# Exponentials on VectorE from three shifted bit lines and by single heads, in an attention block on one core

## The chip, the cores and the metric

The kernel runs on one core of one Trainium2 chip. The metric is the device time of one execution in microseconds. A core has five engines that run their own instruction queues in order and meet through semaphores: TensorE (PE in the profile; its weight loads stand apart as PEld), VectorE (DVE), ScalarE (ACT), GpSimd (POOL) and SyncE (SP, which here only issues DMAs). TensorE writes its results to PSUM, eight banks of 128 partitions x 512 f32; VectorE and ScalarE read them there.

## What is computed

A multi-head attention block: 2048 positions, width 448, 16 heads of 28 values.

```python
B, S, D = x.shape          # 1, 2048, 448
H = 16
Dh = D // H                # 28
qkv = (x @ wqkv).reshape(B, S, 3, H, Dh).transpose(2, 0, 3, 1, 4)
q, k, v = qkv[0], qkv[1], qkv[2]
scores = einsum("bhqd,bhkd->bhqk", q, k) * (Dh ** -0.5)
p = softmax(scores, axis=-1)
o = einsum("bhqk,bhkd->bhqd", p, v)
return o.transpose(0, 2, 1, 3).reshape(B, S, D) @ wo
```

Inputs and output are bf16.

## The kernel before

**Tiling.** Four heads form a group g (G = 4); each head has 32 partitions, 28 for its values and four for helper rows. Queries are cut in four chunks c of 512 (QW), keys in 16 tiles j of 128 (NKT). A *set* is one group with one query chunk: 4 heads x 16 key tiles = 64 score tiles of 128 keys x 512 queries. There are 16 sets, worked off in the order of the list ORDER.

**Scores.** `emit_s` (L599) multiplies a key tile with a query chunk. The contraction is 28 values and some helper rows that subtract a bound of the maximum and fold in a constant, so that the result needs no maximum search. TensorE can be addressed as smaller arrays. A score product uses either the 32 rows of its head i, or 64 rows: two heads' rows, where the query tile QP[c][k][z] holds zeros for the other head of the pair. Heads 0 and 1 lie in rows 0 to 63 (half 0), heads 2 and 3 in rows 64 to 127 (half 1). A *step* is a key tile for two heads, hp and hp + 2, one of each half. If a step is emitted alone, its two products take 64 rows each; if ScalarE's and VectorE's steps are emitted together, all four take 32 rows each (the argument `alone`):

```python
r = slice(2 * HP * k, 2 * HP * (k + 1)) if wide(s, t) and alone else slice(HP * i, HP * (i + 1))
```

**Exponentials.** 512 steps are shared out between two engines. ScalarE takes a step from one of two pairs of banks, "a0" and "a1", with its exponential (`do_exp`, L773) and writes the tile pt in bf16. VectorE takes a step from the pair "d" (`do_a`, L785): it adds a constant to the scaled score and stores 16-bit integers I, whose bits read as bf16 are a power of two with a linear mantissa. For two such steps together (2048 columns) `do_add` (L806) makes two terms: m, from the mantissa bits (an and/or, then a product with I itself), and E, the exponent bits alone. Their sum approximates the exponential, so VectorE's steps give two value products for each head, ScalarE's give one. LOGSUM is the constant that puts both on the same scale.

**Value products.** `do_pv` (L866) multiplies the tile VA (32 columns for each head: 28 values and a column of ones that sums the softmax denominator) with a term and adds it up in bank "o". Head i uses columns 32i to 32i + 31 of the array, so the products of the four heads can run side by side; `waves` (L855) pairs a step of heads 0 and 2 with one of heads 1 and 3.

**After a set** (`finish_set`, L904), bank "o" goes to SBUF, the denominators travel through DRAM by DMA to be inverted and spread, and VectorE multiplies. Output projections run through bank "m", as do the projections of K, Q and V of later groups, spread over the sets by gates that count steps.

**Order.** The program's order is decided when it is built, by a planner in the kernel: it keeps a clock for each engine with estimated durations (D_S = 0.325 us for a score step whatever its tile sizes, D_WAVE for four value products, D_EXP for an exponential), and picks for the engine whose clock is lowest. `pick_pe` (L964) prefers a score step as soon as a bank is free, then value products and projections; where TensorE's recent load is low it inserts products on zeros into "o" or "m" (`dense`, L634). `s_choose` (L657) gives VectorE a step beside ScalarE's if `dve_ok` (L649) says that VectorE would be done before ScalarE; it asks that bank "d" has been free for D_LATE = 0.25 us. On the chip the engines keep the order, not the times.

Of the kernel before, what the change touches and what calls it, by code (L numbers as in the profile page):

```python
# [16 lines left out]
LAT = 0.2  # L17
# [6 lines left out]
D_LATE = 0.25  # L24
# [12 lines left out]
def kernel(  # L37
# [29 lines left out]
    NTERM = 2  # L67
    LOGSUM = 0.5864160
# [25 lines left out]
    VA = [[big.tile([P, GH, XB, P], BF16, name=f"VA{h}_{b}") for b in range(NXB)] for h in range(2)]  # L94
    xs = [big.tile([P, XB, D], BF16, name=f"xs{b}") for b in range(NXB)]
# [78 lines left out]
    res = {"a0": 0.0, "a1": 0.0, "d": 0.0, "o": 0.0, "m": 0.0}  # L174
    ops = {"PE": [], "ACT": [], "DVE": [], "SP": []}
    cnt = {"step": 0}
# [9 lines left out]
    def ready(op):  # L186
        if cnt["step"] < op.gate or (op.acq == "m" and op.gives[0][0] == "O" and left() < 6):
            return None
        r = 0.0
        for n in op.need:  # L190
            if n not in evt:
                return None
            t, e = evt[n]
            r = max(r, t + (0.03 if e == op.eng else LATS.get((e, op.eng), LAT)))
        if op.acq is not None:
            if res[op.acq] is None:
                return None
            r = max(r, res[op.acq])
        return r + op.lag
# [42 lines left out]
    def k_job(g, sc, bank, pri, gate=0, split=2, eng="DVE", epri=None):  # L242
# [3 lines left out]
        def mm(part):  # L246
            if part == 0:
                held[key] = bank_tile(bank) if bank in ("o", "m") else pair_tile(bank)
            mm_proj(held[key][:, 0:QW], 1, g, sc, range(part * n, (part + 1) * n))
# [23 lines left out]
    def kn_job(g, bank, pri, gate=0):  # L273
        key = ("KN", g)

        def mm(sc):
            if sc == 0:
                held[key] = bank_tile(bank) if bank in ("o", "m") else pair_tile(bank)
# [22 lines left out]
    def kn_first(sc, bank, pri):  # L301
        key = ("KN0", sc)

        def mm():
            held[key] = pair_tile(bank)[:, 0:QW]
            nc.tensor.matmul(out=held[key], lhsT=blockK[:], rhs=sqt.pop(("K", 0, sc))[:], start=True, stop=True)
# [23 lines left out]
    def q_job(g, c, bank, pri, gate=0, split=2):  # L330
# [4 lines left out]
        def mm(part):  # L335
            if part == 0:
                held[key] = bank_tile(bank) if bank in ("o", "m") else pair_tile(bank)
            mm_proj(held[key][:, 0:QW], 0, g, c, range(part * n, (part + 1) * n))

        def evac():  # L340
            if first:
                t = qtt[0] = wk.tile([P, QW], BF16, name="qt0", bufs=1)
            else:
                t = QAt[(g, c)] = big.tile([P, QW], BF16, name=f"QA{c}", tag=f"QA{c}", bufs=2)
# [27 lines left out]
    def qn_first(bank, pri):  # L372
        g = c = 0

        def mm():
            held["qn0"] = bank_tile(bank) if bank in ("o", "m") else pair_tile(bank)
# [11 lines left out]
        def join():  # L388
            QAt[(0, 0)] = big.tile([P, QW], BF16, name="QA0", tag="QA0", bufs=2)
# [41 lines left out]
    def v_job(h, kt, bank, pri, gate=0, eng="DVE"):  # L431
# [4 lines left out]
        def mm(part):  # L436
            if part == 0:
                held[key] = bank_tile(bank) if bank in ("o", "m") else pair_tile(bank)
# [20 lines left out]

    def oproj_job(c, tq, pri):  # L460
# [9 lines left out]
        def evac():  # L470
            held[key + ("sb",)] = osb = wk.tile([P, D], BF16, name="osb", bufs=3)
# [57 lines left out]
    for b, bank in enumerate(("a0", "a1", "d", "a0")):  # L529
# [4 lines left out]
    for sc in range(NQC):  # L534
        kn_first(sc, "a1" if sc % 2 == 0 else "d", 1.5)
# [9 lines left out]
    for kt in range(0, NKT, 2):  # L545
        v_job(0, kt, "o" if kt in (0, 4) else "m", 7 + kt, eng="ACT" if kt < 6 else "DVE")
    q_job(0, 1, "m", 16.2)
# [5 lines left out]
    for g in range(1, G):  # L553
        a = (g - 1) * NQC * STEPS + (STEPS + 4 if g == 1 else 6)
        z = g * NQC * STEPS - 34 - (STEPS if g == G - 1 else 0)
# [7 lines left out]
    for kt in range(0, NKT, 2):  # L563
        v_job(1, kt, "m", 150 + kt, a + (z - a) * kt // NKT)
    for c in range(CL):
# [4 lines left out]
    remain = {s: [list(range(NKT)), list(range(NKT))] for s in range(NSET)}  # L570
    todo = sum(len(q) for s in remain for q in remain[s])
    started = set()
# [7 lines left out]

    def set_gc(s):
        return ORDER[s]

    def next_step(hp, s_min=0):
        for s in range(s_min, NSET):
            if remain[s][hp]:
                return s
            if s > cur["s"]:
                return None
        return None  # L590
# [5 lines left out]
    def take(s, hp):  # L596
        return (s, hp, remain[s][hp].pop(0))

    def emit_s(ps, off, step, alone, t):  # L599
        s, hp, j = step  # L600
        g, c = set_gc(s)
        q = QP[c][hp][g % 2] if wide(s, t) else QAt[(0, 0)]
        for k in range(2):
            i = hp + 2 * k
            r = slice(2 * HP * k, 2 * HP * (k + 1)) if wide(s, t) and alone else slice(HP * i, HP * (i + 1))
            nc.tensor.matmul(out=ps[:, (off + k) * QW:(off + k + 1) * QW],  # L606
                             lhsT=KAt[(g, j // XB)][r, (j % XB) * P:(j % XB + 1) * P], rhs=q[r, :],
                             start=True, stop=True, tile_position=(r.start, 0))

# [36 lines left out]
    def exp_tail_est():  # L646
        return max(free["ACT"], 0.0) + D_EXP * (len(exps) + left())

    def dve_ok(t):  # L649
        if res["d"] is None or res["d"] > t - D_LATE:  # L650
            return False
        if chain["cur"] is None and chain["used"] >= NCH:
            return False
        fin = max(free["DVE"], t + 0.5) + 1.14 + 3 * 0.34 + 0.3 + (1.8 if adds else 0.0)
        return fin <= free["ACT"] + D_EXP * (len(exps) + max(0, left() - 2)) + 0.2

    def s_choose(t):  # L657
        s = cur["s"]
        while s < NSET and not remain[s][0] and not remain[s][1]:
            s += 1  # L660
        if s >= NSET:
            return None
        cur["s"] = s
        q = qa_ready(s)
        if q is None or q > t:
            return None
        r = remain[s]
        dstep = astep = None
        if dve_ok(t) and left() >= 4:
            ds, want = d_set(s, t)  # L670
            if ds is not None and remain[ds][want] and r[1 - want]:
                dstep, astep = take(ds, want), take(s, 1 - want)
        if astep is None:
            hp = 0 if len(r[0]) > len(r[1]) else 1 if len(r[1]) > len(r[0]) else cur["half"]
            cur["half"] = 1 - hp
            astep = take(s, hp)
        return (None, astep, dstep)

    def d_set(s, t):
        ch = chain["cur"]  # L680
        if ch is not None:
            cs = ch["steps"][0][0]
            if remain[cs][ch["next"]]:
                return cs, ch["next"]
            if remain[cs][1 - ch["next"]]:
                return cs, 1 - ch["next"]
            return None, None
        n = len(remain[s][0]) + len(remain[s][1])
        if n < DRAIN:
            s += 1  # L690
            if s >= NSET:
                return None, None
            q = qa_ready(s)
            if q is None or q > t:
                return None, None
        r = remain[s]
        return s, (0 if len(r[0]) >= len(r[1]) else 1)

    def do_sd(t):
        s = cur["s"]  # L700
        if s >= NSET or not dve_ok(t) or left() < 4:
            return None
        q = qa_ready(s)
        if q is None or q > t:
            return None
        s, want = d_set(s, t)
        if s is None or not remain[s][want]:
            return None
        end = t + D_S
        put_d(take(s, want), end, True, t)  # L710
        note(t, 512 if wide(s, t) else 256)
        cnt["step"] += 1
        return end

    def put_d(dstep, end, alone, t):
        pd = pair_tile("d")
        emit_s(pd, 0, dstep, alone, t)
        outst[dstep[0]] += NTERM
        res["d"] = None
        if chain["cur"] is None:  # L720
            chain["used"] += 1
            chain["cur"] = {"I": wk.tile([P, 4 * QW], I16, name="I4", bufs=NCH), "steps": [], "sh": [], "open": 0,
                            "next": None, "done": 0}
        ch = chain["cur"]
        ch["steps"].append(dstep)
        ch["next"] = 1 - dstep[1]
        a_fifo.append((end + LATS[("PE", "DVE")], pd, ch, len(ch["steps"]) - 1))
        if len(ch["steps"]) == 2:
            chain["cur"] = None
# [4 lines left out]
    def s_ready():  # L734
        if left() == 0:
# [6 lines left out]
        q = qa_ready(next(s for s in range(NSET) if remain[s][0] or remain[s][1]))  # L742
# [11 lines left out]
    def do_s(t):  # L754
        c = s_choose(t)
        if c is None or c[0] is not None:
            return None
        _, astep, dstep = c
        note(t, 256 if dstep is None and not wide(astep[0], t) else 512)
        bank = s_bank()  # L760
        ps = pair_tile(bank)
        emit_s(ps, 0, astep, dstep is None, t)
        outst[astep[0]] += 1
        res[bank] = None
        end = t + D_S
        exps.append((end + LATS[("PE", "ACT")], ps, bank, astep))
        if dstep is not None:
            put_d(dstep, end, False, t)
        cur["u"] += 1
        cnt["step"] += 1 + (dstep is not None)  # L770
        return end

    def do_exp(t):  # L773
# [6 lines left out]
        pending.append({"step": step, "k": 0, "ap": pt[:], "ready": end + LATS[("ACT", "PE")], "pt": True, "ch": None})  # L780
# [4 lines left out]
    def do_a(t):  # L785
        r, pd, ch, n = a_fifo.pop(0)
        dst = ch["I"][:, n * 2 * QW:(n + 1) * 2 * QW]
        nc.vector.tensor_scalar(out=dst, in0=pd[:], scalar1=BIAS, scalar2=0.0, op0=ALU.add, op1=ALU.max)  # L788
        end = t + 1.135 * SLOW_V
        res["d"] = end + LAT  # L790
        ch["open"] += NTERM
        ch["done"] += 1
        if ch["done"] == 2:
            adds.append([ch, 0, 2, 0])
        elif chain["cur"] is ch and not any(remain[ch["steps"][0][0]]):
            chain["cur"] = None
# [362 lines left out]
```

## Time and profile before

| | |
|---|---|
| median of 3 runs | 405.94 us (404.34 to 407.94) |
| the profiled execution | 405.42 us, span from first to last instruction 403.4 us |
| busy in the span | ScalarE 379.7 us (94%), VectorE 356.3 (88%), TensorE 350.3 (87%), GpSimd 20.0 (5%) |
| instructions | TensorE 3141 matmuls, VectorE 516, ScalarE 422 |
| chain that ended last | ScalarE 57% of the span (its exponential 56%), TensorE 22%, issue 8%, VectorE 7%, DMA 5% |
| granted TensorE clock, mean | 0.984 |

A row of a group reads: line, engine, operation, output<-inputs, shapes, x count | busy time of the group, mean ns of one | idle time of the engine just before them, and what ended it. Instructions of one engine can overlap, so that busy time is less than count times mean. A matmul's shape begins with the rows*columns of the array that it takes. A matmul's recorded length of about 0.385 us contains the time until its results are out; the next one of the same shape can start before that.

### The profile page before, as it was taken

The page shows a single profiled execution, that of the slowest core. Times are in us where ns is not written, and L with a number is a line of the kernel's source. Part 1 is how long each engine was busy: PE and PEld are TensorE (multiplying, and loading weights), DVE is VectorE, ACT ScalarE, POOL GpSimd, SP SyncE. Part 2 cuts the span into 40 slices and gives each one's busy share as a digit, 9 for nine tenths or more (in the row PEclk, how much of TensorE's full clock was granted, in tenths as well). Part 3 has the DMA queues.
Part 4 walks back from the last instruction along what each step waited for, and adds up shares of the span by engine and source line. Part 5 has one row for each costly group of instructions (what it writes and reads, how often), then busy time and mean ns, then how long its engine had stood idle before and what let it go on. Part 6 is the DMA issues. An engine that isn't in the chain of part 4 may idle for free.

```text
span 403.4 us, 7956 instructions
## 1 busy us (share of the span) xinstructions
PE 350.3 (87%) x3141; PEld 117.4 (29%) x3164; DVE 356.3 (88%) x516; ACT 379.7 (94%) x422; POOL 20.0 (5%) x47
## 2 busy tenths in 40 slices
PE   7789888999899989998878989878888898989874
PEld 3343332222333232232222222222222222222222
DVE  1659989999989999999999999898778999999953
ACT  3668999999999999999999999999999999999992
POOL 8730000000000000000000000000000000000000
PEclk9959999999999999999999999999999999999998
DMA  8820001000100000010000001000000010010101
GB/s 270 209 86 7 9 1 52 4 28 23 32 26 4 25 3 26 16 38 27 27 2 27 2 8 54 17 29 0 27 3 8 35 37 28 24 51 23 51 2 47
DMA packets 16077, 13.98 MB, mean 35 GB/s; under 512 B 6076, under 2 KB 13608, under 8 KB 16040
## 3 DMA queue, kind: packets, MB, share of 16 engines
q1 hardware_dynamic: 13704, 11.18, 9.3%
q10 hardware_dynamic: 1824, 1.89, 1.7%
q0 software_dynamic: 512, 0.40, 0.5%
q8 instruction: 25, 0.41, 0.4%
q14 instruction: 12, 0.10, 0.1%
HBM read 7.37 MB, written 1.96 MB: 23 GB/s over the span
## 4 chain that ended last, share of the span: by engine, by line
ACT 57%; PE 22%; issue 8%; DVE 7%; DMA 5%; ACTq 0%; SPq 0%; DVEq 0%
ACT pt L776 56%; PE a L606 9%; PE o L885 4%; DVE I L788 2%; PE m L226 2%; PE m L467 2%; DMA WRAW<-in_wqkv_dram 1%; PE m L441 1%; DMA rr<-scr 1%; DMA QP<-zero 1%; PE d L606 1%; PE o L441 1%; DVE m L819 1%; DVE QA L349 1%; DMA den<-o_sb 0%
## 5 line engine op out<-in xcount | busy, mean ns | idle before, releaser
L776 ACT ACTIVATE pt<-a 128x1024 bf16<-128x1024 f32 x398 | 366.0, 1170 | 4.2 <-PE d L606 1.8
L606 PE MATMUL a<-QP,KA 64*128 64x512 bf16 (+1 forms) x786 | 154.3, 381 | 38.6 <-ACT pt L776 36.7
L788 DVE TENSOR_SCALAR I<-d 128x1024 int16<-128x1024 f32 x114 | 138.4, 1214 | 14.0 <-PE d L606 13.0
L606 PEld LDWEIGHTS <-KA 64*128 64x128 bf16 (+1 forms) x1024 | 57.9, 92 | 173.5 <-issue 170.0
L885 PE MATMUL o<-pt,VA 128*32 128x512 bf16 x796 | 88.6, 385 | 0.7 <-ACT pt L776 0.7
L819 DVE TENSOR_TENSOR m<-m,I 128x2048 bf16<-128x2048 bf16 x57 | 69.4, 1217 | 0.8
L606 PE MATMUL d<-QP,KA 32*128 32x512 bf16 (+1 forms) x224 | 43.8, 383 | 0.0
L814 DVE TENSOR_SCALAR m<-I 128x2048 int16<-128x2048 int16 x57 | 39.1, 686 | 0.6
L823 DVE TENSOR_SCALAR E<-I 128x2048 int16<-128x2048 int16 x57 | 38.9, 682 | 0.0
L885 PEld LDWEIGHTS <-VA 128*32 128x32 bf16 x1252 | 22.2, 94 | 48.3 <-issue 48.3
L226 PE MATMUL m<-XT,WRAW 112*32 112x512 bf16 x464 | 35.7, 384 | 0.5 <-ACT XT L503 0.3
L885 PE MATMUL o<-m,VA 128*32 128x512 bf16 x228 | 33.6, 386 | 0.0
L885 PE MATMUL o<-E,VA 128*32 128x512 bf16 x228 | 32.4, 385 | 0.0
L441 PE MATMUL m<-WRAW,XT 112*128 112x224 bf16 x112 | 16.8, 279 | 0.4 <-DVE VA L452 0.4
L636 PE MATMUL o<-zero 128*128 128x512 bf16 x41 | 14.0, 385 | 1.0 <-issue 1.0
L441 PEld LDWEIGHTS <-XT 112*128 112x128 bf16 x128 | 11.3, 107 | 10.2 <-issue 6.7
L226 PEld LDWEIGHTS <-WRAW 112*32 112x32 bf16 x512 | 8.5, 94 | 16.1 <-issue 13.1
L938 DVE TENSOR_TENSOR xs<-o_sb,rr 128x512 bf16<-128x512 f32 x12 | 8.2, 686 | 5.2 <-DMA rr<-scr 5.1
L258 DVE TENSOR_SCALAR KA<-m,kmask,ones 128x512 bf16<-128x512 f32 x13 | 10.4, 798 | 2.3 <-ACT sq L240 2.0
L349 DVE TENSOR_SCALAR QA<-m,qmask 128x512 bf16<-128x512 f32 x15 | 11.2, 747 | 0.1
L467 PE MATMUL m<-WO,xs 128*128 128x448 bf16 x36 | 11.0, 359 | 0.0
L916 DVE COPY o_sb<-o 128x512 f32<-128x512 f32 x15 | 10.3, 685 | 0.5
(109 smaller groups left out, 156.6 us busy)
## 6 DMA issues: line engine op xcount, KB each, us to landing
rr<-scr SPq DMA_DIRECT2D x15, 256.0 KB
QP<-zero SPq DMA_DIRECT2D x16, 128.0 KB
QP<-QA SPq DMA_DIRECT2D x60, 28.0 KB
xs<-in_x_dram SPq DMA_DIRECT2D x3, 448.0 KB
out_dram<-osb SPq DMA_DIRECT2D x12, 112.0 KB
WRAW<-in_wqkv_dram ACTq DMA_DIRECT2D x3, 392.0 KB
QP<-su SPq DMA_DIRECT2D x30, 2.0 KB
xs<-in_x_dram ACTq DMA_DIRECT2D x1, 448.0 KB
```

The costliest lines, as they stand in the source:

```text
L226: nc.tensor.matmul(out=ps[HP * i:HP * (i + 1), :], lhsT=WRAW[t][:, cc, h * Dh:h * Dh + HP], rhs=XT[c][:, cc, :], start=(cc == 0), stop=(cc ...
L349: nc.vector.tensor_scalar(out=t[:], in0=held[key][:, 0:QW], scalar1=qmask[:, 0:1], scalar2=None, op0=ALU.mult)
L441: nc.tensor.matmul(out=held[key][:, part * w:(part + 1) * w], lhsT=XT[b][:, cc, t * P:(t + 1) * P], rhs=WRAW[2][:, cc, h * w:(h + 1) * w], ...
L467: nc.tensor.matmul(out=held[key][:, 0:D], lhsT=otile(g, c)[:, tq * P:(tq + 1) * P], rhs=WO[:, g, :], start=(g == 0), stop=(g == G - 1))
L606: nc.tensor.matmul(out=ps[:, (off + k) * QW:(off + k + 1) * QW], lhsT=KAt[(g, j // XB)][r, (j % XB) * P:(j % XB + 1) * P], rhs=q[r, :], st ...
L636: nc.tensor.matmul(out=cur["o"][:], lhsT=zero[:, 0:P], rhs=zero[:], start=False, stop=False, skip_group_check=True)
L776: nc.scalar.activation(out=pt[:], in_=ps[:], func=ACT.Exp, scale=LN2 / 128.0)
L788: nc.vector.tensor_scalar(out=dst, in0=pd[:], scalar1=BIAS, scalar2=0.0, op0=ALU.add, op1=ALU.max)
L814: nc.vector.tensor_scalar(out=ch["m"][:, w], in0=src, scalar1=0x7F, scalar2=0x3F00, op0=ALU.bitwise_and, op1=ALU.bitwise_or)
L819: nc.vector.tensor_tensor(out=mv, in0=mv, in1=src.bitcast(BF16), op=ALU.mult)
L823: nc.vector.tensor_scalar(out=ch["E"][:, w], in0=src, scalar1=0x7F80, scalar2=None, op0=ALU.bitwise_and)
L885: nc.tensor.matmul(out=o[HP * i:HP * (i + 1), :], lhsT=vt[:, gg, j % XB, HP * i:HP * (i + 1)], rhs=e["ap"][:, k * QW:(k + 1) * QW], start= ...
```

## The change

VectorE's exponential is now made of three terms: I itself read as bf16, and I with 43 and with 85 added (SHIFT), which shifts the linear mantissa line. Each is multiplied with its own copy of V, scaled by the weights WT = 1, 201/256 and 159/256; the copies VS are made by VectorE (`vs_job`), 16 tiles of 128x1024. So two additions take the place of three operations for four score tiles, and there are three value products instead of two.

VectorE now takes single heads, not steps of two, in two banks "d0" and "d1" of 512 columns instead of one pair "d". Up to two such heads go out beside a step of ScalarE. Four heads of one chain are evicted one by one (`do_a`, 128x512) and then shifted together (`do_add`, 128x2048). ScalarE's step takes one head of each half, whichever have most left. A head's tile in `emit_s` has 64 rows if no other product of the group lies in its half, and 32 rows otherwise. Value products are put together by single heads, one of each of the four (`waves`). D_LATE is replaced by D_SOON = 0. Some gates move (projections for group 1 start at step 16 instead of 36; each group's end 56 steps before its last instead of 34), QA keeps one buffer instead of two, and the transposed blocks of x use "a0" and "a1" only.

```diff
-    NTERM = 2
-    LOGSUM = 0.5864160
+    SHIFT = (0, 43, 85)
+    WT = (1.0, 201.0 / 256.0, 159.0 / 256.0)
+    NTERM = len(SHIFT)
+    LOGSUM = 1.6305015
...
+    def vs_job(h, b, pri):
+        def scale(k):
+            nc.vector.tensor_scalar(out=VS[k - 1][h][b][:].rearrange("p g t e -> p (g t e)"),
+                                    in0=VA[h][b][:].rearrange("p g t e -> p (g t e)"),
+                                    scalar1=WT[k], scalar2=None, op0=ALU.mult)
...
-    for b, bank in enumerate(("a0", "a1", "d", "a0")):
+    for b, bank in enumerate(("a0", "a1", "a0", "a1")):
         xt_job(b, bank, 0.1 * b)
...
-        a = (g - 1) * NQC * STEPS + (STEPS + 4 if g == 1 else 6)
-        z = g * NQC * STEPS - 34 - (STEPS if g == G - 1 else 0)
+        a = (g - 1) * NQC * STEPS + (16 if g == 1 else 6)
+        z = g * NQC * STEPS - 56 - (STEPS if g == G - 1 else 0)
...
+    def emit_s(items, t):
+        halves = [i // 2 for _, (_, i, _) in items]
+        total = 0
+        for out_ap, (s, i, j) in items:
+            g, c = set_gc(s)
+            w = wide(s, t)
+            x = i // 2
+            q = QP[c][i % 2][g % 2] if w else QAt[(0, 0)]
+            r = slice(2 * HP * x, 2 * HP * (x + 1)) if w and halves.count(x) == 1 else slice(HP * i, HP * (i + 1))
+            total += r.stop - r.start
+            nc.tensor.matmul(out=out_ap, lhsT=KAt[(g, j // XB)][r, (j % XB) * P:(j % XB + 1) * P], rhs=q[r, :],
+                             start=True, stop=True, tile_position=(r.start, 0))
+        note(t, total * QW // P)
...
+    def d_banks(t):
+        return sorted((b for b in ("d0", "d1") if res[b] is not None and res[b] <= t + D_SOON), key=lambda b: res[b])
...
     def do_s(t):
...
+        got = d_more(s, t, True) if left() >= 16 or chain["cur"] is not None else []
+        used = {g[2][1] for g in got}
+        step = []
+        for x in range(2):
+            own = [i for i in (2 * x, 2 * x + 1) if i not in used and remain[s][i]]
+            step.append(take(s, max(own, key=lambda i: (len(remain[s][i]), (i + cur["u"]) % 2))))
         bank = s_bank()
         ps = pair_tile(bank)
-        emit_s(ps, 0, astep, dstep is None, t)
+        emit_s([(ps[:, k * QW:(k + 1) * QW], step[k]) for k in range(2)] + [(g[1][:], g[2]) for g in got], t)
...
     def do_a(t):
-        r, pd, ch, n = a_fifo.pop(0)
-        dst = ch["I"][:, n * 2 * QW:(n + 1) * 2 * QW]
+        r, b, pd, step, ch, n = a_fifo.pop(0)
+        dst = ch["I"][:, n * QW:(n + 1) * QW]
         nc.vector.tensor_scalar(out=dst, in0=pd[:], scalar1=BIAS, scalar2=0.0, op0=ALU.add, op1=ALU.max)
...
     def do_add(t):
+        ch, m, k = adds[0]
+        w = slice(0, m * QW)
+        r = ch[k] = wk.tile([P, HG * QW], I16, name=f"J{k}", bufs=NCH)
+        nc.vector.tensor_scalar(out=r[:, w], in0=ch["I"][:, w], scalar1=float(SHIFT[k]), scalar2=None, op0=ALU.add)
...
     def waves(c):
-        A = [e for e in c if e["step"][1] == 0]
-        B = [e for e in c if e["step"][1] == 1]
-        n = min(len(A), len(B))
-        full = [(A[k], B[k]) for k in range(n)]
-        rest = [(e,) for e in (A[n:] + B[n:])]
+        by = [[e for e in c if e["step"][1] == i] for i in range(HG)]
+        n = min(len(q) for q in by)
+        full = [tuple(q[k] for q in by) for k in range(n)]
+        by = [q[n:] for q in by]
+        rest = []
+        while any(by):
+            rest.append(tuple(q.pop(0) for q in by if q))
         return full, rest
```

`d_more` (new) picks the heads for VectorE: for each free bank of "d0" and "d1" one head, alternating between the two halves, if `dve_ok` allows it.

## The prediction, made before the changed kernel ran

> **What bounds the kernel now.** I read the busy times first, then the kernel by stages, then the costliest groups, then the waits, and last the order in time around single score products. By stages (columns: stretch, its length, busy time and count of each engine, the granted clock, DMA):
>
> ```profile
> core 0: us, PE busy (x) PEld busy (x) DVE busy (x) ACT busy (x) POOL busy (x), PEclk, DMA share, GB/s
> 0.00:21.90 21.90, 15.77 (x171) 8.15 (x173) 10.04 (x54) 10.29 (x14) 18.13 (x44) 1.00 0.78 223
> 21.90:33.00 11.10, 11.10 (x64) 4.65 (x64) 7.14 (x10) 7.96 (x11) 1.84 (x4) 0.54 0.25 75
> 33.00:391.30 358.30, 317.68 (x2876) 101.95 (x2896) 335.83 (x446) 357.15 (x390) 0.00 (x0) 1.00 0.07 22
> 391.30:403.40 12.10, 5.72 (x39) 2.60 (x38) 3.27 (x8) 4.26 (x8) 0.00 (x0) 0.89 0.12 39
> ```
>
> The main stage is 33.0 to 391.3. ScalarE is busy there for 357.2 of 358.3 us: it is the bound. VectorE has 22.5 us idle, TensorE 40.6. The groups behind it:
>
> ```profile
> L776 ACT ACTIVATE pt<-a 128x1024 bf16<-128x1024 f32 x398 | 366.0, 1170 | 4.2 <-PE d L606 1.8
> L606 PE MATMUL a<-QP,KA 64*128 64x512 bf16 (+1 forms) x786 | 154.3, 381 | 38.6 <-ACT pt L776 36.7
> L788 DVE TENSOR_SCALAR I<-d 128x1024 int16<-128x1024 f32 x114 | 138.4, 1214 | 14.0 <-PE d L606 13.0
> L819 DVE TENSOR_TENSOR m<-m,I 128x2048 bf16<-128x2048 bf16 x57 | 69.4, 1217 | 0.8
> L814 DVE TENSOR_SCALAR m<-I 128x2048 int16<-128x2048 int16 x57 | 39.1, 686 | 0.6
> L823 DVE TENSOR_SCALAR E<-I 128x2048 int16<-128x2048 int16 x57 | 38.9, 682 | 0.0
> ```
>
> An exponential of ScalarE costs 366.0/398 = 0.92 us (they overlap, so not the mean of 1.17). TensorE's idle time is nearly all waiting for ScalarE to free a score bank. So an exponential moved off ScalarE gains 0.92 us, as long as the other two engines have room.
>
> What TensorE pays when two neighbouring matmuls use different tile shapes (rows*columns of the array, the first pair of numbers of a form) is in the order in time (start, length; "[...]" is idle time before it):
>
> ```profile
> 202.40 0.39 PE L606 MATMUL a<-QP,KA 64*128 64x512 bf16 x2
> ...
> 202.72 0.09 PEld L606 LDWEIGHTS <-KA 32*128 32x128 bf16 x1 [0.23 <-issue]
> ...
> 203.33 0.39 PE L606 MATMUL d<-QP,KA 32*128 32x512 bf16 x2
> 203.64 0.09 PEld L606 LDWEIGHTS <-KA 64*128 64x128 bf16 x1 [0.23 <-issue]
> ...
> 205.47 0.11 PEld L636 LDWEIGHTS <-zero 128*128 128x128 bf16 x2 [0.23 <-issue]
> 205.47 0.60 PE L636 MATMUL o<-zero 128*128 128x512 bf16 x2
> ...
> 208.82 0.39 PE L606 MATMUL a<-QP,KA 64*128 64x512 bf16 x2
> 209.03 0.39 PE L606 MATMUL d<-QP,KA 64*128 64x512 bf16 x2
> ```
>
> Matmuls of one shape on different rows start together (x2 in one line of 0.39); of one shape on the same rows, 0.21 apart (208.82, 209.03). Where the shape changes, even the weight load is held: 0.32 after 202.40 and 0.31 after 203.33, when the last matmul's results are nearly out. At 205.47 two loads of one shape for the whole array pass in 0.11, the second long before the first matmul ends, so rows in use do not hold a load; the change of shape does. Once no wait for ScalarE hides it:
>
> ```profile
> 32.71 0.39 PE L606 MATMUL d<-QP,KA 32*128 32x512 bf16 x2
> 33.02 0.10 PEld L606 LDWEIGHTS <-KA 64*128 64x128 bf16 x2 [0.23 <-issue]
> 33.03 0.39 PE L606 MATMUL a<-QP,KA 64*128 64x512 bf16 x2
> ```
>
> The next shape starts 0.32 after the last one. Before, neighbouring score products change between 32 and 64 rows 18 times in the whole program, and nearly always while TensorE waits for ScalarE anyway.
>
> **The change, part by part.** Counts are from the order of the two programs' instructions.
>
> ScalarE: 398 exponentials become 376. Gain 22 x 0.92 = 20.2 us where it is the bound: the main stage would be 338.1.
>
> VectorE: removed 114 evictions and 57 chains of three (138.4 + 39.1 + 69.4 + 38.9 = 285.8). Added 272 evictions of 128x512, 136 additions and 16 scaled copies of V. The new eviction is not in the trace; below, half a present one (0.607), above, L258's 0.798, which has two per-partition scalars. I take L382's 0.683 (same shape, a constant scalar): 185.8. An addition reads and writes 2048 16-bit values as L814 and L823 do: 136 x 0.684 = 93.0. A scaled copy lies between L412 (512 values, 0.293) and L814 (2048): 0.42 x 16 = 6.7. Sum 285.5: VectorE works as long as before, 336 in the main stage (315 to 367 at the two ends). The new multiplications stand ahead of value products that need them, in the first set and mid-kernel, with evictions queued behind them: 6.7 us in all, inside that sum.
>
> TensorE, value products: 1252 become 1568, of three terms instead of two. Put together into passes of four that run side by side, 328 become 406: 78 x 0.215 (two passes start 0.21 to 0.22 apart) = +16.8. Score products, taking each group as running side by side: 432 passes to 377, -11.8. Fillers on zeros: 66 to 33, -7.1. Changes of shape between groups: 9 more at 0.32 - 0.215 = 0.105, +0.9. The four nearly cancel: need of the main stage 317.7 - 1.2 = 316.5.
>
> TensorE, the new mix of shapes: this is the term that decides. With one single head for VectorE, the half that shares it goes in 32-row tiles, and the other half still in a 64-row tile (the expression for r in emit_s). Of the 376 score groups that feed ScalarE, 111 are in order 64, 32, 32 rows and 110 are 32, 64, 32. Before, a group with VectorE in it was all of one shape. So inside groups there are 111 + 2 x 110 = 331 new changes of shape, on rows that do not overlap. That last point the trace never shows: each of its changes of shape meets rows in use. Bounds: nothing, if disjoint rows run side by side; above, 0.36, the start-to-start from value products into 64-row scores (204.79 to 205.15; 119.2 us). I take 0.32, the row at 33.03, because the load was held by the shape and not by the rows: 331 x 0.32 = 105.9 us. Need of the main stage: 316.5 + 105.9 = 422.4.
>
> The Trainium skill, "TensorEngine Tiling (Array Packing)", section Tiling Modes (Key Properties), says that changing the mode, not just the tile, drains TensorE. On overlapping rows this trace agrees (0.31 to 0.32); on disjoint rows no run shows it yet. By that rule the sum is as above.
>
> Waits: a mixed score group now waits for ScalarE's pair and for one or two banks of VectorE with no margin (0.25 before). Behind it on TensorE's queue stand the value products and the next scores. Before, no wait of TensorE for VectorE shows at L606 d; with 336 us of VectorE work in 422 I price this at nothing. If TensorE were not longer, there would be no cover: then up to the 13.0 us that VectorE now waits at L788 is the size to expect.
>
> The rest: the four transposed blocks of x on two pairs instead of three. At 9.86 and 11.87 the pairs have been free since 7.9 and 10.7: nothing. Single buffers for QA, rewritten a whole group of sets later, and the shared last output tiles: nothing. SyncE issues the same 168 instructions and GpSimd the same work; no DMA is moved past another that someone waits for.
>
> Sum: 33.0 before the main stage + 422.4 + 12.1 behind it = 467.5. TensorE can run only two score pairs ahead of ScalarE, so a stretch without VectorE's heads (127 groups are plain pairs) goes at 0.92 a group even where TensorE needs less. Pricing the order by the rows above, with 0.92 as floor over every four or every two groups, adds 5.8 or 9.8: I take 7. Span 474.5. The profiled execution took 405.42 with a span of 403.4, so 2.0 more: 476. That run is 0.5 under the median of 405.94, which is left out.
>
> **Rivals.** (1) *Disjoint rows run side by side after all.* TensorE then needs 316.5 of 338.1 and the gain stays; VectorE with 336 has no room left and part of its 13.0 us of waiting comes back: 403.4 - 20.2 = 383 to 396, I take 390, time 392, faster. For it: tiles are independent within a shape, starting 0.00 to 0.01 apart. Against it: the held weight load. The point that decides: a change inside a group is free up to (338.1 - 316.5)/331 = 65 ns, and above (358.3 - 316.5)/331 = 126 ns the kernel is slower than before; the trace has 0.10 more than a pass even where the new rows had to wait for a pass anyway, and 0.32 where a pass is added.
> "TensorE: Matmul & The Clock Gate", Part 3 (The mechanism), also of the Trainium skill, speaks for this rival: loads for non-conflicting row groups are pulled ahead and such matmuls run concurrently. It says nothing of mixed sizes.
>
> (2) *VectorE becomes the bound.* Without the drain, at 0.798 an eviction, VectorE needs 367 in the main stage: 33 + 367 + 12 + 2 = 414, slower by 2%. Against it: L382 at 0.683. With the drain, 367 stays under 422.
>
> (3) *The drain is dearer or VectorE's banks also stall TensorE:* 0.36 for each change gives 435.7; with 10 of floors and some waiting, 493 to 498. This lies inside the forecast's range. That the change does not do what it says is out: the counts show it.
>
> **Numbers.** Drain 0.88; rival 1 0.09; rival 2 0.02; something near no change 0.01. Time 476. Range: below, 0.31 a change without floors gives 466, and 3% less need of TensorE than its busy time shows 452; above, 498. It holds 9 in 10 of the drain's cases, 0.81 in all, and leaves the rivals out. Measurements here tell 1% (404.3 to 407.9). Faster 0.09, same 0.01, slower 0.90.
>
> **What would show it.** Right: TensorE without gaps in the main stage, ScalarE waiting for TensorE at its exponential, mean score groups of two or three steps 0.32 apart, weight loads of the 64-row tile about 0.31 after a 32-row matmul of the same group, VectorE idle by some 90 us. Wrong: the three matmuls of a mixed group starting together. Also wrong in size if evictions of 128x512 are far from 0.683, or if the changes cost nearer 0.22 or 0.36.

## The result and the profile after

| | before | after |
|---|---|---|
| median | 405.76 us (404.34 to 407.94, 4 runs) | 455.39 us (454.02 to 484.78, 4 runs) |
| profiled execution, span | 405.42 us, 403.4 us | 454.02 us, 452.0 us |

The ratio is 1.1207, 95% interval 1.113 to 1.1283: slower by 12%. One of the four runs after, 484.78 us, had a mean granted clock of 0.917 where the others had 0.996 to 0.999; the ratio leaves it out.

The stages of the changed kernel, with the columns as before (stretch, its length, busy time and count of each engine, clock, DMA):

```profile
21.90:33.00 11.10, 10.92 (x100) 4.78 (x98) 10.08 (x21) 10.15 (x14) 1.30 (x3) 1.00 0.25 73
33.00:440.00 407.00, 396.32 (x3109) 111.50 (x3122) 328.33 (x573) 354.93 (x365) 0.00 (x0) 1.00 0.07 19
440.00:452.00 12.00, 6.86 (x56) 2.87 (x54) 4.56 (x10) 4.96 (x9) 0.00 (x0) 0.97 0.13 40
```

The main stage grew from 358.3 to 407 us, and TensorE (first number of a stretch) is now busy for 396 of them. ScalarE and VectorE have 52 and 79 us idle. What they wait for stands in the costliest groups:

```profile
L801 ACT ACTIVATE pt<-a 128x1024 bf16<-128x1024 f32 x376 | 367.0, 1032 | 53.6 <-PE d L620 36.1
L816 DVE TENSOR_SCALAR I<-d 128x512 int16<-128x512 f32 x272 | 184.1, 687 | 66.5 <-PE d L620 64.2
L620 PE MATMUL a<-QP,KA 64*128 64x512 bf16 (+1 forms) x742 | 211.0, 384 | 8.5 <-ACT pt L801 6.5
L839 DVE TENSOR_SCALAR J<-I 128x2048 int16<-128x2048 int16 x136 | 90.0, 682 | 0.4
```

The direction of the waiting has turned: TensorE waits 6.5 us for ScalarE instead of 36.7, and ScalarE waits 53.6 us before its exponential, nearly all of it for score products. The order in time inside two mixed score groups (a 64-32-32 group, then a 32-64-32 group) shows why:

```profile
200.28 0.09 PEld L620 LDWEIGHTS <-KA 64*128 64x128 bf16 x1 [0.42 <-issue]
200.29 0.70 PE L620 MATMUL a<-QP,KA 64*128 64x512 bf16 x2
...
200.60 0.09 PEld L620 LDWEIGHTS <-KA 32*128 32x128 bf16 x2 [0.23 <-issue]
200.61 0.39 PE L620 MATMUL d<-QP,KA 32*128 32x512 bf16 x1
...
201.47 0.09 PEld L620 LDWEIGHTS <-KA 32*128 32x128 bf16 x1 [0.42 <-issue]
201.47 0.70 PE L620 MATMUL a<-QP,KA 32*128 32x512 bf16 x2
...
201.79 0.09 PEld L620 LDWEIGHTS <-KA 64*128 64x128 bf16 x1 [0.23 <-issue]
202.10 0.09 PEld L620 LDWEIGHTS <-KA 32*128 32x128 bf16 x1 [0.23 <-issue]
202.11 0.38 PE L620 MATMUL d<-QP,KA 32*128 32x512 bf16 x1
```

The tiles of a group lie on different rows, and yet each change of size holds the next weight load by 0.31 to 0.32 us. The second group needs three steps, from 201.47 to 202.11, where three tiles of one size start together. (The two "a" products of 0.70 us are one of each size, merged into one line.)

### The profile page after: what moved, and what is told of

Same layout as the page of the kernel before. It is cut to its first block, busy times and chain, and to the rows that moved or that the text cites. A ratio compares the mean times of both kernels' runs of the same rounds, so it can differ in the third digit from the quotient of the medians.

```text
span 452.0 us, 8710 instructions
## 1 busy us (share of the span) xinstructions
PE 429.9 (95%) x3426; PEld 127.2 (28%) x3447; DVE 353.0 (78%) x655; ACT 380.3 (84%) x400; POOL 20.0 (4%) x47
## 4 chain that ended last, share of the span: by engine, by line
PE 82%; ACT 10%; issue 3%; DMA 2%; DVE 2%; ACTq 0%; SPq 0%
PE a L620 38%; PE o L899 21%; ACT pt L801 9%; PE d L620 8%; PE m L230 6%; PE m L481 3%; PE m L445 2%; DMA WRAW<-in_wqkv_dram 1%; DMA QP<-zero 1%; PE m L283 1%; PE o L650 1%; ACT sq L244 0%; ACT XT L517 0%; PE m L407 0%; DVE kp L315 0%
## 5 line engine op out<-in xcount | busy, mean ns | idle before, releaser
L801 ACT ACTIVATE pt<-a 128x1024 bf16<-128x1024 f32 x376 | 367.0, 1032 | 53.6 <-PE d L620 36.1
L816 DVE TENSOR_SCALAR I<-d 128x512 int16<-128x512 f32 x272 | 184.1, 687 | 66.5 <-PE d L620 64.2
L620 PE MATMUL a<-QP,KA 64*128 64x512 bf16 (+1 forms) x742 | 211.0, 384 | 8.5 <-ACT pt L801 6.5
L620 PEld LDWEIGHTS <-KA 32*128 32x128 bf16 (+1 forms) x1024 | 67.6, 91 | 217.5 <-issue 215.4
L899 PE MATMUL o<-pt,VA 128*32 128x512 bf16 x752 | 107.4, 385 | 0.6 <-ACT pt L801 0.3
L620 PE MATMUL d<-QP,KA 32*128 32x512 bf16 (+1 forms) x267 | 93.9, 384 | 0.0
L839 DVE TENSOR_SCALAR J<-I 128x2048 int16<-128x2048 int16 x136 | 90.0, 682 | 0.4
L899 PE MATMUL o<-J,VS 128*32 128x512 bf16 x544 | 75.6, 385 | 0.5 <-issue 0.5
L899 PE MATMUL o<-I,VA 128*32 128x512 bf16 x272 | 64.3, 386 | 0.5 <-DVE I L816 0.3
L899 PEld LDWEIGHTS <-VS 128*32 128x32 bf16 x544 | 16.9, 94 | 18.0 <-issue 17.8
L445 PEld LDWEIGHTS <-XT 112*128 112x128 bf16 x128 | 10.2, 97 | 7.7 <-issue 7.0
L456 DVE CAST VA<-m 128x224 bf16<-128x224 f32 x26 | 8.9, 383 | 1.6 <-PE m L445 1.3
```

Of the source, the lines that this page charges most:

```text
L445: nc.tensor.matmul(out=held[key][:, part * w:(part + 1) * w], lhsT=XT[b][:, cc, t * P:(t + 1) * P], rhs=WRAW[2][:, cc, h * w:(h + 1) * w], ...
L456: nc.vector.tensor_copy(out=dst, in_=src)
L620: nc.tensor.matmul(out=out_ap, lhsT=KAt[(g, j // XB)][r, (j % XB) * P:(j % XB + 1) * P], rhs=q[r, :], start=True, stop=True, tile_position ...
L801: nc.scalar.activation(out=pt[:], in_=ps[:], func=ACT.Exp, scale=LN2 / 128.0)
L839: nc.vector.tensor_scalar(out=r[:, w], in0=ch["I"][:, w], scalar1=float(SHIFT[k]), scalar2=None, op0=ALU.add)
L899: nc.tensor.matmul(out=o[HP * i:HP * (i + 1), :], lhsT=vt[:, gg, j % XB, HP * i:HP * (i + 1)], rhs=e["ap"], start=(SETMM[key] == 1), stop= ...
```

## The experiments

Three kernels were run first: the changed one with the mix of sizes removed, the changed one with fewer changes of size, and the kernel before with nothing but the mix.

**One shape.** Order, engines, counts and terms are those of the changed kernel; only the rows of tiles differ. The 64-row tile reads zeros for its second head, so the products are the same.

```diff
             r = slice(2 * HP * x, 2 * HP * (x + 1)) if w and halves.count(x) == 1 else slice(HP * i, HP * (i + 1))
             total += r.stop - r.start
+            if len(items) > 2:
+                r = slice(HP * i, HP * (i + 1))
```

> The changed kernel with the same order of instructions, but every score group that holds a head for VectorE takes 32-row tiles throughout: 7 changes between 32 and 64 rows are left of 345. Theory (each change of tile shape inside a group costs TensorE 0.32 us): TensorE loses 338 x 0.32 = 108 us of need, falls under ScalarE's 376 x 0.92 = 346 us, and the time drops to 385 to 398 us, below the kernel before. Rival A (the time went into the three value products or into waiting for VectorE's single banks): it stays above 440 us. Rival B (VectorE becomes the bound once TensorE is out of the way): 398 to 415 us.

Measured: 384.04 us (381.88 to 384.80), ratio to before 0.9494 (0.9431 to 0.9558). The main stage, and a mixed group in order of time:

```profile
33.00:370.00 337.00, 315.89 (x3169) 96.90 (x3165) 320.51 (x577) 336.15 (x367) 0.00 (x0) 1.00 0.08 23
```

```profile
200.24 0.10 PEld L622 LDWEIGHTS <-KA 32*128 32x128 bf16 x3 [0.42 <-issue]
200.25 0.39 PE L622 MATMUL a<-QP,KA 32*128 32x512 bf16 x2
200.25 0.38 PE L622 MATMUL d<-QP,KA 32*128 32x512 bf16 x1
```

Three loads and three matmuls start together. ScalarE is the bound again, busy 336.2 of 337 us. The time is just under the range expected. Against the changed kernel 71 us are gone, all of the loss and more: against the kernel before, run beside it at 403.84 us, the gain is 19.8 us, close to the 22 x 0.92 = 20.2 us of the exponentials that left ScalarE. Both rivals fall: neither the third value product nor VectorE's single banks add time to the path here.

**Wide tile first.** Inside a group the 64-row product is emitted first.

```diff
         halves = [i // 2 for _, (_, i, _) in items]
+        items = sorted(items, key=lambda it: -(halves.count(it[1][1] // 2) == 1))
         total = 0
```

> The changed kernel with the same order of groups, but inside a group the 64-row product goes first, so 32-64-32 becomes 64-32-32: 245 changes between 32 and 64 rows instead of 345, on the same rows with the same work. Theory: 100 x 0.32 = 32 us less, 423 us, or up to 435 where ScalarE's 0.92 us a group is the floor. Rival (the cost is that of mixing sizes in a group at all, or lies elsewhere): 450 to 457 us as before.

Measured: 430.16 us (424.68 to 430.87), ratio 1.062 (1.0524 to 1.0716). The same tiles on the same rows in another order save 25 us, 0.25 for each change taken out (the two kernels were not run side by side). It is the change of size that costs, not the presence of two sizes in a group. Part of what is missing to 0.32 is clock: the runs near the median have a mean granted clock of 0.980 to 0.982, the fastest run 0.994, and that run, 424.68 us, is 29 us under the 454.02 of the changed kernel.

**Before, with mixed shapes.** In every step that is emitted alone, the second product takes 32 rows, the first keeps 64.

```diff
-            r = slice(2 * HP * k, 2 * HP * (k + 1)) if wide(s, t) and alone else slice(HP * i, HP * (i + 1))
+            r = slice(2 * HP * k, 2 * HP * (k + 1)) if wide(s, t) and alone and k == 0 else slice(HP * i, HP * (i + 1))
```

> The kernel before, with nothing of the change but its mix of shapes: where a step is emitted alone, its first product takes 64 rows and its second only its own 32 rows, so that 349 steps get a change of shape between disjoint rows. Work, order and waits are the same. Theory: 349 x 0.32 = 112 us more for TensorE, of which its 40.6 us of waiting in the main stage take up a part: some 70 us more, 465 to 490 us. Rival (it is another part of the change that costs): 404 to 408 us as before.

Measured: 711.05 us (708.09 to 712.65), ratio 1.7595 (1.7501 to 1.7689). The direction is the theory's, the size is far outside. The stages tell what came on top (the clock is the number after GpSimd's):

```profile
33.00:84.00 51.00, 49.92 (x375) 14.70 (x374) 41.20 (x60) 45.66 (x47) 0.00 (x0) 1.00 0.05 14
100.00:600.00 500.00, 498.85 (x2030) 90.10 (x2029) 240.86 (x312) 277.98 (x273) 0.00 (x0) 0.50 0.04 11
```

Until 84 us the clock is full; then it is halved and stays so until 657 us, although TensorE is busy for 99.8% of the time from 100 to 600 us by the profile. At half clock a change of shape takes longer too (0.53 from the start of the 64-row product at 301.09 to the weight load of the next at 301.62):

```profile
301.08 0.10 PEld L606 LDWEIGHTS <-KA 64*128 64x128 bf16 x1 [0.84 <-issue]
301.09 1.14 PE L606 MATMUL a<-QP,KA 64*128 64x512 bf16 x2
...
301.62 0.10 PEld L606 LDWEIGHTS <-KA 32*128 32x128 bf16 x1 [0.44 <-issue]
```

So this run doesn't price a change of shape. Two smaller doses do: the same edit in every fourth and in every second of these steps.

```diff
         q = QP[c][hp][g % 2] if wide(s, t) else QAt[(0, 0)]
+        cnt["alone"] = cnt.get("alone", 0) + alone
+        cut = alone and cnt["alone"] % 4 == 0
         for k in range(2):
             i = hp + 2 * k
-            r = slice(2 * HP * k, 2 * HP * (k + 1)) if wide(s, t) and alone else slice(HP * i, HP * (i + 1))
+            r = slice(2 * HP * k, 2 * HP * (k + 1)) if wide(s, t) and alone and not (cut and k) else slice(HP * i, HP * (i + 1))
```

> The kernel before with the mix of shapes (64 rows, then 32 on other rows) in every fourth step that is emitted alone: 122 changes between 32 and 64 rows instead of 18. Theory (a price per change, hidden as far as TensorE waits for ScalarE): 104 x 0.32 = 33 us of TensorE's 40.6 us of waiting are used up, the time rises by little, 404 to 414 us, and the granted clock stays near 1. Rival (mixing sizes drops the clock by itself, whatever the amount): the clock falls to 0.5 for long stretches and the time is above 450 us.

> As the quarter, but in every second step that is emitted alone: 227 changes instead of 18. Theory: 209 x 0.32 = 67 us against 40.6 us of waiting, so 26 us and the unevenness more, 425 to 445 us, if the clock stays up. If the clock is lost because drains make the array idle too often, it should be lost here in part: up to 600 us, with the clock between 0.6 and 0.9. Rival (no price per change): 404 to 408 us.

Measured: a quarter 414.32 us, ratio 1.0244 (1.0172 to 1.0316); half 428.89 us, ratio 1.065 (1.0556 to 1.0744). The main stage of each, a quarter first:

```profile
33.00:400.00 367.00, 338.34 (x2885) 98.76 (x2900) 337.09 (x447) 362.07 (x390) 0.00 (x0) 1.00 0.07 21
```

```profile
33.00:410.00 377.00, 355.60 (x2836) 100.88 (x2854) 335.90 (x442) 363.96 (x385) 0.00 (x0) 1.00 0.07 21
```

The clock is 1.00 over the main stage of both, so mixing sizes doesn't drop it by itself. The price per change is there: 10 us for 104 changes (the range expected ended at 10), 25 us for 209. A part of the 10 us is clock again, since the runs near the median have a mean of 0.982; the fastest runs, at a mean of 0.997 and 0.998, took 410.26 and 425.94 us, where the kernel before took 403.06 at 0.997. TensorE's idle time sinks from 40.6 to 28.7 and 21.4 us; it is not used up before the time rises. That it lies in other places than the changes do is the likely reason.

**All narrow.** What do the 64-row tiles buy? In the one-shape kernel they are left in the groups for ScalarE alone. Here they go too.

```diff
-            if len(items) > 2:
-                r = slice(HP * i, HP * (i + 1))
+            r = slice(HP * i, HP * (i + 1))
```

> The one-shape kernel with 32-row tiles also in the score groups that feed ScalarE alone, so no score product takes 64 rows. No change between 32 and 64 rows is left; same order, same number of passes. Theory: 64 rows buy nothing but array activity; time as with one shape, 380 to 388 us, if the clock holds. Rival (the clock follows the rows in use): the granted clock falls below 0.9 and the time is above 410 us.

Measured: 380.28 us (379.58 to 385.34), ratio 0.9409 (0.9371 to 0.9447), the fastest of all kernels here; the profiled run has the clock at 1.00 throughout. That it is better than one shape is not shown: the intervals overlap, and the clock differs. Its first three runs have a mean of 0.993 to 1.000, those of one shape 0.982 to 0.994; at 0.982 the two took 385.34 and 384.80 us.

**More on VectorE.** Does the one-shape kernel leave VectorE room? Its durations in the planner were put lower (0.54 instead of 0.6 us for an eviction, 0.56 instead of 0.62 in `dve_ok`, 0.04 instead of 0.068 as the fixed part of an addition).

> The one-shape kernel with VectorE's durations put lower in the planner, so that it gives it more: 368 exponentials on ScalarE instead of 376, 288 evictions instead of 272. Theory if ScalarE is the bound there: 8 x 0.92 = 7 us less, 377 us. Rival (VectorE, 320.5 of 337 us busy in the one-shape kernel, has no room for 16 x 0.687 + 8 x 0.687 = 16.5 us more): 383 to 392 us.

Measured: 385.49 us (382.39 to 388.23), ratio 0.9518 (0.9438 to 0.9598): the rival. In the main stage VectorE (332.58) is now as busy as ScalarE (331.09):

```profile
33.00:372.00 339.00, 317.65 (x3185) 93.15 (x3202) 332.58 (x605) 331.09 (x359) 0.00 (x0) 0.99 0.08 23
```

So eight exponentials more on VectorE gained nothing: with 376 on ScalarE the two engines are close enough to balance.

**What took the clock away.** From the recorded starts two shares can be estimated for a stretch: the time in which any matmul streams, and the part of the array that streams (the same time, weighted with rows x columns of the tile over 128 x 128). A matmul of 512 columns is taken to stream for 0.213 us, because two on the same rows start 0.209 apart (64-row products, median) or 0.216 (value products) in the trace of before; one of fewer columns is taken in proportion.

| kernel, stretch at full clock | some matmul streams | part of the array | clock |
|---|---|---|---|
| before, main stage | 0.62 | 0.58 | held |
| one shape | 0.67 | 0.59 | held |
| all narrow | 0.66 | 0.53 | held |
| before, half mixed | 0.67 | 0.52 | held |
| changed kernel | 0.70 | 0.50 | held in three of four runs |
| before, mixed, 23 to 84 us | 0.70 | 0.46 | lost at 84 us; mean 0.576 to 0.582 in all four runs |

(The expectation below says 0.63 and 0.72 of the first and the last stretch.) The kernel that lost it has matmuls in flight most of the time, but the smallest part of the array at work. To separate the two, the kernel before was run with 32-row tiles in every score product (no change of size, fewer rows), alone and with more fillers on zeros.

```diff
-            r = slice(2 * HP * k, 2 * HP * (k + 1)) if wide(s, t) and alone else slice(HP * i, HP * (i + 1))
+            r = slice(HP * i, HP * (i + 1))
```

and for the second kernel also, in `do_s` and `do_sd`,

```diff
-        note(t, 256 if dstep is None and not wide(astep[0], t) else 512)
+        note(t, 256 if dstep is None else 512)
...
-        note(t, 512 if wide(s, t) else 256)
+        note(t, 256)
```

> The kernel before with 32-row tiles in every score product: same order, no change between 32 and 64 rows, half the array's rows in use in the steps emitted alone. It asks what took the clock away in the kernel before with mixed shapes. If the gate goes by the part of the array that streams (rows x columns, mean 0.58 before, 0.46 with mixed shapes at full clock, 0.50 in the changed kernel): here it is about 0.48, so the clock drops in part or in full, time above 420 us. If it goes by drains or by the time in which anything streams (0.63 before, 0.72 with mixed shapes): the clock holds and the time is that of before, 401 to 406 us.

> As the one above, but the planner is told that such a step loads half as many rows, so that it puts in 125 products on zeros instead of 76; two exponentials fewer on ScalarE. If the share of the array in use is what holds the clock, it holds here, 401 to 408 us; if not, this is the same as the one above.

Measured: the first took 422.48 us in the median, but 406.21 to 441.47 from run to run, with a mean granted clock of 0.982 to 0.859; no ratio was formed. The second took 403.72 us (401.23 to 408.00), ratio 0.9981 (0.9937 to 1.0024). The clock of the first in 40 slices of its profiled run, in tenths, and a stretch of it:

```profile
PEclk9955558655995699999998999999999996899988
150.00:350.00 200.00, 177.12 (x1588) 53.82 (x1584) 183.29 (x240) 197.99 (x216) 0.00 (x0) 0.98 0.06 18
```

and the clock of the second:

```profile
PEclk9999999999999999999999999999999999999599
```

In the first it comes and goes, with no change of size between 32 and 64 rows at all. Between 150 and 350 us of that run the part of the array is 0.47, about that of the mixed kernel; here the clock falls only twice, for 3.4 us each. With fillers the part is 0.52, and the clock holds but for one fall of 10.2 us at 371.6. So in these kernels the loss of the clock goes with a small part of the array at work, not with the time in which anything streams: by that column the wide-first kernel (0.70, with 0.55 of the array) would have lost it with the mixed one, and the narrow one (0.60) would not. That the part of the array is the cause is likely, not shown: the kernel with fillers also has two exponentials fewer on ScalarE and another order.

The means are not a threshold either. The shortest stretch at one clock in any of these traces is 3.4 us. In the 3.4 us before each of the nine falls within a main stage, the part of the array was 0.31 to 0.38, while a matmul was streaming for 0.41 to 0.69 of the time. Cut into such stretches, the main stage of before has none under 0.40. But the changed kernel's profiled run has eight at 0.38 or less, down to 0.33, and kept its clock. Nor does the share say when the clock comes back: in the mixed kernel at half clock, from 100 to 600 us, two passes start 0.39 us apart (median), so that the part of the array is about 0.49, more than the 0.46 at which the clock was lost, and yet it stayed down. What the gate counts stays open. For the 64-row tiles with their zeros no gain but clock shows here: all narrow, which has none, is no slower than one shape.

## Why the prediction was right

**The mechanism** was the first case, and each link is shown. A change between 32 and 64 rows costs a drain (the next load waits until the product ahead is nearly out) even on rows that do not overlap: the median start to start between neighbouring score products of different size, worked out from the recorded starts, is 0.317 us from 32 to 64 and 0.319 from 64 to 32, against 0.32 taken. The Trainium skill's rule in "TensorEngine Tiling (Array Packing)", Tiling Modes (Key Properties), that a change of mode drains TensorE, holds here for disjoint rows too. What rival 1 took from the Trainium skill, "TensorE: Matmul & The Clock Gate", Part 3 (The mechanism), holds here only among tiles of one size: there the loads are pulled ahead (three at 200.24 in the one-shape kernel), across sizes they are not (200.60 in the changed one, 0.31 after the product at 200.29).

**The terms.** For the changes inside groups 105.9 us were priced. Over the whole program, changes between the two sizes take 116.0 us from start to start after and 17.9 before: 98 us more. (The traces show 351 and 21 of them, the programs' order has 345 and 18; some records of other matmuls between them are missing. Most of the 21 wait for ScalarE.) VectorE's prices were right: an eviction of 128x512 takes 687 ns (0.683 taken), an addition 682 (0.684). VectorE has 79 us idle in the main stage (some 90 forecast), and no wait of TensorE for VectorE's banks shows, as priced.

**The size that was off.** 476 was forecast and 455 measured, inside the range. The prediction counted 429.4 us from 33.0 to the last score group, which now starts at 440.7, so 407.7. The step that failed is "need of the main stage 317.7 - 1.2 = 316.5": it took TensorE's busy time of before as its need. From value products or other work into a score group, start to start, the median is 0.358 before and 0.312 after, and the sums over these 329 and 336 places are 120.8 and 107.1 us: 13.7 us of the old busy time were not need. The extra lies between the weight load and its matmul, as in the kernel before (first pair) and the changed one (second pair):

```profile
202.35 0.14 PEld L606 LDWEIGHTS <-KA 64*128 64x128 bf16 x2 [0.42 <-issue]
202.40 0.39 PE L606 MATMUL a<-QP,KA 64*128 64x512 bf16 x2
...
204.15 0.09 PEld L620 LDWEIGHTS <-KA 64*128 64x128 bf16 x2 [0.42 <-issue]
204.16 0.39 PE L620 MATMUL a<-QP,KA 64*128 64x512 bf16 x2
```

That is 0.05 apart before and 0.01 after. The cause is a late release by ScalarE, and the recorded starts and ends show it. The first product of a group goes into the pair of banks that the exponential two back has read. In the main stage of before, 262 of 321 such products start 0.05 us after that exponential's end, and they come 0.358 after the work ahead of them (medians); where the exponential had ended earlier it is 0.312. In the changed kernel it is the same 0.357 and 0.312, but only 61 of 326 products are late. The profile counts these short waits as TensorE's busy time, and most of them vanish when TensorE is the bound.

Another 5 us lie between 21.9 and 33.0, and they are luck: the clock was 0.54 there in the profiled run before, which the prediction took over, and 1.00 in the one after, so that 100 matmuls were done there instead of 64 (11.1 x 0.46 = 5.1 us of work). Other runs of the kernel before have a mean clock of up to 1.000. The remaining 3 us were not traced. The range held the result because its lower end allowed TensorE 3% less need than its busy time; without that its lower end was 466. (3% of the need at 0.31 a change, 419.1 us, is 12.6, which gives 454 and not the 452 of the forecast; 455 lies inside both.)

**Rival 1** was what the one-shape kernel then did, and its price was off the other way: 392 forecast, 384 measured. The 13.0 us that VectorE waited for score products came back as 9.8 at its new eviction, but beside ScalarE's work, not on the path. **Rival 2** rested on 0.798 for an eviction, which takes 0.687; only with 16 evictions more does VectorE come level with ScalarE, and at 385 us, not 414.

**Not foreseen:** that the mix comes close to costing the clock as well. The run of the changed kernel with a clock of 0.917, at 484.78 us, is what that looks like.

## What to carry to other kernels

When small matmuls are packed side by side, use one tile size in a run of them, and change the size only where TensorE is waiting anyway: here a change cost 0.32 us, on rows in use and on others alike, which is 0.1 us more than a pass of 0.21 and takes away the overlap. A busy engine's time is not its need: waits of a few tens of nanoseconds inside it (0.05 us here) can vanish when the bound moves, and idle time on average is no cover for work that falls elsewhere. Undo the one suspect line before giving up a change: the rest of this one was worth 5% to 6%.

## What was not expected of the hardware

The granted clock can go to half with TensorE busy 98% of the span: in the kernel before with mixed shapes it fell at 84 us and stayed at 0.50 for most of the 711 us. In the runs here the loss goes with the part of the array that streams (lost at 0.46, coming and going at 0.47, lost in one of four runs at 0.50, held at 0.52 and above but for one fall of 10 us), not with the time in which matmuls are in flight (0.70 where it was lost, 0.62 where it was held). Part 1 of "TensorE: Matmul & The Clock Gate" in the Trainium skill ties the gate to how busy TensorE is and to idle windows. The fall at 84 us does not fit that: TensorE was busy for 99% of the 3.4 us before it.

A weight load into rows that are not in use waits for the drain too, if its tile size differs from the last one's (0.31 us at 200.60 in the changed kernel). Loads of one size pass at once, even for rows in use (two for the whole array within 0.11 us at 205.47 in the kernel before).
